# Two small products in separate slots with one PSUM bank each, and the output products spread over six slots

## Chip, cores, metric

One core of a Trainium2 chip. The metric is the device time of one launch in microseconds (us), median of several runs. The experiments ran in several rounds, on more than one chip; each ratio below is to the kernel before in the same rounds.

## The reference, cut

An attention block with 32 inducing points feeds a gated feed-forward layer with a gated residual. `B, N, C = 4, 12416, 128`, `d_ff = 1536`.

```python
h = mab(I, x)                 # 32 summaries of each batch
x = mab(x, h)                 # each token mixes the 32 rows of h
g, val = x @ w_gate, x @ w_val
ffn_out = (gelu(g) * val) @ w_out
out = x + sigmoid(x @ w_res) * ffn_out
```

The kernel never forms the second `x`: it multiplies the attention weights `rt` of each token with matrices that already hold `h @ w_gate`, `h @ w_val`, `h @ w_res` and `h`. What is called a **mix** below is the product of `rt` with the last two: the gate mix gives the argument of the sigmoid, the residual mix gives `x` itself.

## The kernel before

Work goes in groups of 512 tokens. A full group has six **slots**; in each, PE makes two gate halves and two value halves (128 x 512 each), ACT puts a gelu over each gate half, and DVE multiplies 128 x 1024 gelus with the values (`u`). Forty-eight **output products** (128 x 128) then sum `u @ w_out` in one bank, two to seven slots behind the group's start. The last DVE step (`th`) closes the group, POOL adds the residual, and a transfer writes the result.

The eight PSUM banks: three in a ring for gate halves, mixes and small work (`bank_g`), two pairs for values (`bank_v`), one for the output sum (`bank_f`).

```python
p_fin = ctx.enter_context(tc.tile_pool(name="fin", bufs=2))        # th and at
ps_g = ctx.enter_context(tc.tile_pool(name="psg", bufs=3, space=bass.MemoryType.PSUM))
ps_v = ctx.enter_context(tc.tile_pool(name="psv", bufs=2, space=bass.MemoryType.PSUM))
ps_f = ctx.enter_context(tc.tile_pool(name="psf", bufs=1, space=bass.MemoryType.PSUM))
...
def mix(self):
    banks = bank_g(), bank_g()
    n = self.tw
    for k in range(self.nk):
        for r, bank in zip((slice(0, 64), slice(64, 128)), banks):
            pe.matmul(bank[:, k * P:(k + 1) * P],
                      rt_t[self.b, self.k][r, self.j0 + k, :], hra_t[self.b][r, :],
                      start=True, stop=True)
    ...
    act.activation(self.th[:, :n], banks[0][:, :n], AC.Tanh, bias=0.0, scale=0.5)
    ...
    act.activation(self.at[:, :n], banks[1][:, :n], AC.Copy, bias=0.0, scale=1.0)

def end(self):
    ve.scalar_tensor_tensor(self.th[:, :tw], self.th[:, :tw], 1.0,
                            self.ffn.rearrange("p k c -> p (k c)")[:, :tw], AL.add, AL.mult)
    po.tensor_tensor(self.at[:, :tw], self.at[:, :tw], self.th[:, :tw], AL.add)
    ...                                            # sy.dma_start(out..., self.at...)
...
# f: the group's first slot; START, MIDDLE (default), END, LATE order the work behind one slot
at(f + 2, lg.mix, START)
for i, n in enumerate((10, 10, 10, 9, 9)):
    at(f + 3 + i, lambda lg=lg, n=n: lg.mms(n))    # output products
at(f + 7, lg.end, LATE)
```

Beside this runs background work for the next batch: twice per batch a burst of exponentials, after one of which up to 40 accumulation products stand in the slot of the mixes of several groups. The gelus run ahead of the values by some gate halves, their lead; a burst uses it up, and the groups after it make 13 gelus instead of 12 until it has grown again.

The softmax here doesn't subtract the row's maximum and nothing guards it: scores larger than these inputs give would overflow.

## Time and profile before

| | before |
|---|---|
| time, first three runs | 882.23 us (881.86 to 885.05) |
| span of the profiled run | 883.8 us |
| busy: PE, DVE, ACT, POOL | 89%, 90%, 89%, 43% |
| period of a plain group (12 gelus) | 7.85 us, 32 groups |
| period while the gelus' lead grows (13 gelus) | 8.17 us, some 22 groups |
| period with accumulation | 8.66 us |

A period is the time from one start of the last DVE step (L394) to the next, read from the trace; each group has one. The page's slices (40 equal parts of the span, tenths of busy time; PEclk is the clock granted to PE) show where PE ran below full speed:

```profile
PE   5789989999989999899988999999998899999997
...
POOL 2438884112388776111267877311238531111111
PEclk9689989999999999999999999999999899999999
```

The sixth digit of PEclk (110 to 132 us) is an 8, and so is one near 690 us: stretches of half clock. POOL has 8s in slices 4 to 6 (66 to 132 us), while it converts the next batch, and again in slices 12, 13, 23 and 31.

### The profile page before, as it was taken

The page shows a single profiled execution, that of the slowest core. Times are in us where ns is not written, and L with a number is a line of the kernel's source. Part 1 is how long each engine was busy: PE and PEld are TensorE (multiplying, and loading weights), DVE is VectorE, ACT ScalarE, POOL GpSimd, SP SyncE. Part 2 cuts the span into 40 slices and gives each one's busy share as a digit, 9 for nine tenths or more (in the row PEclk, how much of TensorE's full clock was granted, in tenths as well). Part 3 has the DMA queues.
Part 4 walks back from the last instruction along what each step waited for, and adds up shares of the span by engine and source line. Part 5 has one row for each costly group of instructions (what it writes and reads, how often), then busy time and mean ns, then how long its engine had stood idle before and what let it go on. Part 6 is the DMA issues. An engine that isn't in the chain of part 4 may idle for free.

```text
span 883.8 us, 23924 instructions
## 1 busy us (share of the span) xinstructions
PE 787.8 (89%) x9586; PEld 447.7 (51%) x9586; DVE 794.0 (90%) x773; ACT 782.3 (89%) x1462; POOL 380.6 (43%) x376
## 2 busy tenths in 40 slices
PE   5789989999989999899988999999998899999997
PEld 4544445555554445555545544555555454444444
DVE  8679979799799999889888999979979799999998
ACT  5589979799899999889999999989989799999995
POOL 2438884112388776111267877311238531111111
PEclk9689989999999999999999999999999899999999
DMA  8327884001237976100116877200123521101111
GB/s 306 108 76 154 201 191 93 25 26 38 43 78 155 172 196 137 42 26 25 55 38 131 184 182 160 73 36 26 37 43 74 98 62 37 37 26 37 37 37 40
DMA packets 118991, 78.27 MB, mean 89 GB/s; under 512 B 97216, under 2 KB 99936, under 8 KB 118880
## 3 DMA queue, kind: packets, MB, share of 16 engines
q1 hardware_dynamic: 116592, 74.32, 34.4%
q10 hardware_dynamic: 2288, 2.43, 1.0%
q8 instruction: 75, 1.23, 0.6%
q14 instruction: 36, 0.29, 0.1%
HBM read 27.87 MB, written 25.43 MB: 60 GB/s over the span
## 4 chain that ended last, share of the span: by engine, by line
PE 56%; ACT 23%; DVE 13%; issue 4%; DMA 2%; POOL 1%; ACTq 0%; POOLq 0%; SPq 0%; DVEq 0%
PE f L373 25%; PE g L336 22%; ACT ge L342 17%; DVE u L350 10%; ACT th L388 4%; PE v L336 3%; PE g L157 2%; DVE lo L121 2%; ACT at L390 1%; DMA out_dram<-at 1%; DVE hi L119 1%; PE g L175 1%; POOL at L397 1%; PE g L177 1%; ACT L342 0%
## 5 line engine op out<-in xcount | busy, mean ns | idle before, releaser
L350 DVE TENSOR_TENSOR u<-ge,v 128x1024 bf16<-128x1024 f32 x584 | 702.0, 1215 | 71.6 <-PE v L336 33.6
L342 ACT ACTIVATE ge<-g 128x512 f32<-128x512 f32 x1164 | 622.2, 601 | 51.6 <-PE v L336 20.6
L336 PE MATMUL g<-rt,hgv 64*128 64x512 f16 x1152 | 363.1, 386 | 35.9 <-ACT th L388 15.0
L336 PE MATMUL v<-rt,hgv 64*128 64x512 f16 x1152 | 378.6, 389 | 0.4 <-DVE u L350 0.4
L373 PE MATMUL f<-wO,u 128*128 128x128 bf16 x4656 | 350.8, 223 | 1.0 <-DVE th L394 1.0
L373 PEld LDWEIGHTS <-u 128*128 128x128 bf16 x4656 | 267.6, 99 | 165.9 <-issue 164.5
L397 POOL TENSOR_TENSOR at<-at,th 128x512 f32<-128x512 f32 (+1 forms) x100 | 123.7, 1237 | 430.1 <-ACT ge L342 250.1
L336 PEld LDWEIGHTS <-hgv 64*128 64x128 bf16 x2400 | 102.1, 94 | 151.9 <-issue 83.5
L283 POOL TENSOR_TENSOR a<-eb,z 128x1024 f16<-128x1024 f32 (+1 forms) x49 | 90.9, 1862 | 7.3 <-DMA rt<-a 5.5
L384 PE MATMUL g<-hra,rt 64*128 64x128 f16 x768 | 57.6, 218 | 36.1 <-ACT ge L342 31.4
L121 POOL TENSOR_TENSOR lo<-xf,hi 128x1024 f16<-128x1024 f32 x36 | 76.8, 2134 | 0.3
L384 PEld LDWEIGHTS <-rt 64*128 64x128 f16 x768 | 37.3, 94 | 73.9 <-issue 62.7
L394 DVE SCALAR_TENSOR_TENSOR th<-th,f 128x512 f32<-128x512 f32 (+1 forms) x100 | 66.4, 664 | 1.0 <-PE f L373 1.0
L388 ACT ACTIVATE th<-g 128x512 f32<-128x512 f32 (+1 forms) x100 | 58.5, 585 | 5.8 <-PE g L384 5.5
L390 ACT ACTIVATE at<-g 128x512 f32<-128x512 f32 (+1 forms) x100 | 58.1, 581 | 6.1 <-DMA out_dram<-at 5.0
L119 POOL CAST hi<-xf 128x1024 f16<-128x1024 f32 x36 | 37.3, 1037 | 30.3 <-DMA xf<-in_x_dram 26.1
L157 PEld LDWEIGHTS <-xt 128*128 128x128 f16 x768 | 23.3, 98 | 12.1 <-issue 11.7
L137 ACT ACTIVATE xt<-g 128x1024 f16<-128x1024 f16 x12 | 12.3, 1023 | 13.7 <-PE g L136 13.5
L136 PE MATMUL g<-identF,hi 128*128 128x128 f16 x96 | 10.7, 278 | 10.1 <-DVE hi L119 9.9
L261 POOL TENSOR_TENSOR zt<-zt 128x256 f32<-128x256 f32 (+5 forms) x36 | 15.0, 417 | 2.8
L161 ACT ACTIVATE eb<-g 128x512 f32<-128x512 f32 x18 | 9.8, 597 | 5.2 <-PE g L157 5.2
L136 PEld LDWEIGHTS <-hi 128*128 128x128 f16 x96 | 7.9, 125 | 12.4 <-DVE hi L119 12.4
(104 smaller groups left out, 249.0 us busy)
## 6 DMA issues: line engine op xcount, KB each, us to landing
out_dram<-at SPq DMA_DIRECT2D x96, 256.0 KB, 2.1
xf<-in_x_dram SPq DMA_DIRECT2D x42, 512.0 KB, 4.1
ge<-in_x_dram SPq DMA_DIRECT2D x6, 512.0 KB, 6.0
rt<-a SPq DMA_TRANSPOSE x49, 3.1
xt<-hi SPq DMA_TRANSPOSE x36, 3.5
ge<-in_moe_w_gate_dram ACTq DMA_DIRECT2D x1, 512.0 KB, 4.7
ge<-in_moe_w_val_dram ACTq DMA_DIRECT2D x1, 512.0 KB, 5.6
ge<-in_moe_w_out_dram ACTq DMA_DIRECT2D x1, 512.0 KB, 4.3
```

What stands on the lines that cost most here:

```text
L119: e_hi.tensor_copy(hi[:, :w, :], xf[:, :w, :])
L121: e_lo.tensor_tensor(lo[:, :w, :P], xf[:, :w, :], hi[:, :w, :], AL.subtract)
L283: po.tensor_tensor(a2[:, :n], ev[:, o:o + n, :].unsqueeze(2).to_broadcast([P, n, Q, M]), z[:, o:o + n].unsqueeze(2).unsqueeze(3).to_broadc ...
L336: pe.matmul(*t[n], start=True, stop=True)
L342: act.activation(ge_t[i][:, h * TOK:h * TOK + n], gb[:, :n], AC.Gelu, bias=0.0, scale=1.0)
L350: ve.tensor_tensor(u[:, :n], ge_t.pop(i)[:, :n], v_t.pop(i)[:, :n], AL.mult)
L373: pe.matmul(self.ffn[:, k, :], u_t[self.gi, si][:, o:o + P], wO[:, fc, :], start=first, stop=not self.todo, skip_group_check=True)
L384: pe.matmul(bank[:, k * P:(k + 1) * P], rt_t[self.b, self.k][r, self.j0 + k, :], hra_t[self.b][r, :], start=True, stop=True)
L388: act.activation(self.th[:, :n], banks[0][:, :n], AC.Tanh, bias=0.0, scale=0.5)
L390: act.activation(self.at[:, :n], banks[1][:, :n], AC.Copy, bias=0.0, scale=1.0)
L394: ve.scalar_tensor_tensor(self.th[:, :tw], self.th[:, :tw], 1.0, self.ffn.rearrange("p k c -> p (k c)")[:, :tw], AL.add, AL.mult)
L397: po.tensor_tensor(self.at[:, :tw], self.at[:, :tw], self.th[:, :tw], AL.add)
```

## The change

The intent: each mix takes one bank of the ring at a time, so that PE need not wait for two; and the slot of the gate mix, now shorter, takes four of the output products, one slot behind the last output products of the group before. Background work goes ahead of output products.

```diff
-        def mix(self):
-            banks = bank_g(), bank_g()
+        def mix(self, rows):
+            bank = bank_g()
             for k in range(self.nk):
-                for r, bank in zip((slice(0, 64), slice(64, 128)), banks):
-                    pe.matmul(...)
+                pe.matmul(bank[:, k * P:(k + 1) * P], rt_t[self.b, self.k][rows, self.j0 + k, :],
+                          hra_t[self.b][rows, :], start=True, stop=True)
+            return bank[:, :self.tw]
+        def gate(self):       # Tanh of self.mix(slice(0, 64)) into self.th
+        def residual(self):   # Copy of self.mix(slice(64, 128)) into self.at
...
-        at(f + 2, lg.mix, START)
+        at(f + 2, lg.gate, START)
-            for i, n in enumerate((10, 10, 10, 9, 9)):
-                at(f + 3 + i, lambda lg=lg, n=n: lg.mms(n))
+            for i, n in enumerate((4, 9, 9, 7, 9, 10)):
+                at(f + 2 + i, lambda lg=lg, n=n: lg.mms(n), END)
+            at(f + 5, lg.residual, START)
...
-        def bg(g, p, f, where=END):
+        def bg(g, p, f, where=MIDDLE):
```

(Cut: the bodies of `gate` and `residual`, told in the comments; the one-block groups, where the residual goes to `f + 3`; and one `START` of the background work that became the default.)

More of the change, by code (lines that the diff above doesn't have):

```diff
@@ L376, in mms @@
                     del u_t[self.gi, si]
-        def mix(self):
-            banks = bank_g(), bank_g()
-            n = self.tw
+        def mix(self, rows):
+            bank = bank_g()
             for k in range(self.nk):
-                for r, bank in zip((slice(0, 64), slice(64, 128)), banks):
-                    pe.matmul(bank[:, k * P:(k + 1) * P],
-                              rt_t[self.b, self.k][r, self.j0 + k, :], hra_t[self.b][r, :],
-                              start=True, stop=True)
+                pe.matmul(bank[:, k * P:(k + 1) * P], rt_t[self.b, self.k][rows, self.j0 + k, :],
+                          hra_t[self.b][rows, :], start=True, stop=True)
+            return bank[:, :self.tw]
+        def gate(self):
             self.th = p_fin.tile([P, TOK], FP32, name="th", tag="th")
-            act.activation(self.th[:, :n], banks[0][:, :n], AC.Tanh, bias=0.0, scale=0.5)
+            act.activation(self.th[:, :self.tw], self.mix(slice(0, 64)), AC.Tanh,
+                           bias=0.0, scale=0.5)
+        def residual(self):
             self.at = p_fin.tile([P, TOK], FP32, name="at", tag="at")
-            act.activation(self.at[:, :n], banks[1][:, :n], AC.Copy, bias=0.0, scale=1.0)
+            act.activation(self.at[:, :self.tw], self.mix(slice(64, 128)), AC.Copy,
+                           bias=0.0, scale=1.0)
         def end(self):
@@ L515 @@
         f = first[gi]
-        at(f + 2, lg.mix, START)
+        at(f + 2, lg.gate, START)
         if len(groups[gi][4]) == 6:
-            for i, n in enumerate((10, 10, 10, 9, 9)):
-                at(f + 3 + i, lambda lg=lg, n=n: lg.mms(n))
+            for i, n in enumerate((4, 9, 9, 7, 9, 10)):
+                at(f + 2 + i, lambda lg=lg, n=n: lg.mms(n), END)
+            at(f + 5, lg.residual, START)
             at(f + 7, lg.end, LATE)
         else:
-            at(f + 3, lambda lg=lg: lg.mms(len(lg.todo)))
+            at(f + 3, lg.residual, START)
+            at(f + 3, lambda lg=lg: lg.mms(len(lg.todo)), END)
             at(f + 3, lg.end, LATE)
@@ L552, in plan @@
             bg(19, 2, lambda: turn_h(nb))
-            bg(19, 4, lambda: first_layer_t(nb, 0), START)
+            bg(19, 4, lambda: first_layer_t(nb, 0))
             bg(20, 2, lambda: first_layer_t(nb, 1))
```

## The prediction

> **What bounds the kernel now.** I read the page's busy shares first, then the list of waits, then the starts of the last DVE step of each group (L394), one per 512-token group, and last the timeline of single groups.
>
> ```profile
> PE 787.8 (89%) x9586; PEld 447.7 (51%) x9586; DVE 794.0 (90%) x773; ACT 782.3 (89%) x1462; POOL 380.6 (43%) x376
> ```
>
> Three engines at 89 to 90% do not say which is the bound: back-to-back durations overlap. In order of start, ACT steps of 0.6 us follow each other every 0.477 to 0.494 us, and u products of 1.22 us every 1.137 us where nothing is waited for. So a group (12 gelus, two evictions; 6 u, one L394) could take 12 x 0.485 + 2 x 0.485 = 6.8 us on ACT and 6 x 1.137 + 0.597 = 7.42 us on DVE. Between two L394 starts I measure 7.85 us in 32 groups, about 8.17 us in some 22 (there the kernel makes 13 gelus per group to rebuild its lead), 8.66 us in 15 (accumulation beside them), and more around the bursts. Neither engine is at its floor: something with waits paces both.
>
> ```profile
> PE g L384 <- ACT ge L342: 32.6, 98, 0.4
> PE g L336 <- ACT th L388: 15.0, 69, 0.4
> ACT at L390 <- DMA out_dram<-at: 5.0, 4, 1.9
> ```
>
> The list of waits names the suspect: PE waits for ACT at the mixes (L384), once for nearly each of the 100 groups, and then for the gate's eviction (L388). The timeline of a 7.85 us group, PE then ACT then DVE, shows the loop:
>
> ```profile
> 328.54 0.39 PE L336 MATMUL g<-rt,hgv 64*128 64x512 f16 x1
> ...
> 329.08 0.68 PE L373 MATMUL f<-wO,u 128*128 128x128 bf16 x9
> 329.69 0.39 PE L336 MATMUL g<-rt,hgv 64*128 64x512 f16 x1
> ...
> 329.91 0.38 PE L336 MATMUL g<-rt,hgv 64*128 64x512 f16 x1
> ...
> 330.13 0.22 PE L384 MATMUL g<-hra,rt 64*128 64x128 f16 x1
> 330.76 0.38 PE L384 MATMUL g<-hra,rt 64*128 64x128 f16 x7 [0.41 <-ACT ge L342]
> 331.25 0.37 PE L336 MATMUL g<-rt,hgv 64*128 64x512 f16 x1
> ...
> 331.85 0.37 PE L336 MATMUL g<-rt,hgv 64*128 64x512 f16 x1 [0.21 <-ACT th L388]
> ...
> 332.17 0.73 PE L373 MATMUL f<-wO,u 128*128 128x128 bf16 x10
> 332.83 0.39 PE L336 MATMUL g<-rt,hgv 64*128 64x512 f16 x1
> ```
>
> ```profile
> 331.20 0.60 ACT L388 ACTIVATE th<-g 128x512 f32<-128x512 f32 x1
> 331.69 0.59 ACT L390 ACTIVATE at<-g 128x512 f32<-128x512 f32 x1
> ```
>
> ```profile
> 330.41 0.68 DVE L394 SCALAR_TENSOR_TENSOR th<-th,f 128x512 f32<-128x512 f32 x1
> ```
>
> Call slots by place: p0 to p5, p2 the slot of the mixes. Three g banks turn in a ring. At 330.13 the first mix has its bank; the second needs the bank whose gelu ends only at 330.70, so seven products go at 330.76. The next two gate products need the bank of the last gelu (331.19, product at 331.25) and that of th (331.79, product at 331.85). From the p2 start (329.69) to the p4 start (332.83) PE spends 3.14 us; the other four slots run without a wait, 1.202 us with 10 output products and 1.147 with 9: 2 x 1.202 + 2 x 1.147 = 4.70. Sum 7.84, which is the group. PE and ACT in a loop through the banks set the pace, and the two mixes together close that loop.
>
> **What the skill says.** "TensorE: Matmul & The Clock Gate", section "Wait — 56ns, not 53.3ns?": 128 columns warm take 55.6 ns start to start. The trace agrees: a tenth product lengthens a slot by 1.202 - 1.147 = 0.055 us. Same page, "What's actually happening": after about one idle window of 3.4 us the array runs at half rate. Here shorter stretches of waits suffice (next part but one). "PSUM — Partial Sum Buffer", "Terms": two engines may not use a bank in the same partitions at once; so the matmul must wait for the evicting ACT step, as seen. "Perfetto Trace Analysis", "DVE / Act Engine Instruction": the spread of a semaphore comes after the shown end; the trace has 0.06 us (331.79 to 331.85).
>
> **The change, part by part.** The numbers of instructions stay; table loads too (14 in both ACT orders).
>
> *One bank at p2.* The gate mix takes the free bank and goes at once. The residual mix sits in p5, whose third bank is free by then: its gelu began a slot earlier. ACT's second eviction moves out of p2/p3; ACT has slack (6.8 of 7.85).
>
> *Unpaired mixes.* Eight products in two row halves ran beside each other; now 4 and 4. I choose 4 x 0.055 + 0.1 for the changeover = 0.32 us each. The one in p2 lies inside a new wait; the one in p5 is on the path.
>
> *Four output products in p2.* The f bank is single. They must wait for L394 of the group before, which stands on DVE behind the u of p1. That is the new loop. From the p1 start: u starts 0.73 later (328.54 to 329.27), L394 1.137 after that, lasts 0.68, semaphore 0.06; four products and the changeover 4 x 0.055 + 0.115 = 0.335. So p3 starts at 2.94. Then p3 and p4 with 9 products, 1.147 each; p5 with residual and 7: 0.54 + 0.32 + 0.115 + 0.385 = 1.36; p0 with 9: 1.147. Sum 2.94 + 4.80 = 7.74. Without the wait PE would need 1.20 (p1) + 1.20 (p2: 0.54 + 0.32 + 0.335) + 4.80 = 7.20, so some 0.54 us of waiting replaces the old 0.41 + 0.21 and their surroundings. DVE's next u after L394 hides most of it: v of p3 is ready at 2.94 + 0.73 = 3.67, DVE free at 3.60.
>
> So the 7.85 groups gain 0.11. Those with 13 gelus have an unpaired gate product in p1, +0.22: 7.96, for 8.17, gain 0.21. With accumulation (0.7 us, now between gate and outputs, so that it fills the new wait): p2 starts at 1.42, gate ends 2.28, accumulation about 3.1, outputs 3.5, then 4.80: 8.3 for 8.66, gain 0.36.
>
> *The later residual eviction.* at is written three slots (3.6 us) later, so its two buffers have that much longer until the output transfer lands. Today this wait is rare but dear:
>
> ```profile
> 116.96 0.73 PE L373 MATMUL f<-wO,u 128*128 128x128 bf16 x10
> 119.14 0.58 PE L336 MATMUL g<-rt,hgv 64*128 64x512 f16 x1 [1.45 <-ACT at L390]
> ...
> 120.17 1.25 PE L373 MATMUL f<-wO,u 128*128 128x128 bf16 x10
> ```
>
> ACT waited 1.9 us for the transfer, PE 1.45, and then ten products took 1.25 us and not 0.73: the clock had halved, for 6.8 us. That group took 12.20 us, 4.35 over 7.85. Three others sit where the same wait appears, over 7.85 or 8.17 as their neighbours: the one at 685 us loses 4.6, those at 265 and 474 us 0.5 and 1.0. Together 10.4 us. I credit three quarters, 7.8, because th still waits for POOL, whose add of the group two before ended at 115.87, just when th began (115.98); with a faster pace that wait may appear.
>
> Sum: 32 x 0.11 = 3.5; 22 x 0.21 = 4.6; 15 x 0.36 = 5.4; nine groups next to the bursts, at 8.66 to 8.9, 0.25 each = 2.2; stalls 7.8; the six bursts, where the residual no longer holds a bank ahead of the exponentials, 2. Together 25.5, so 882.2 - 25.5 = 857 us.
>
> **Rivals.** *The new wait equals the old.* If u and L394 answer later, or the unpaired mix costs 0.45, the loop is 7.9 and only the stalls and the accumulating groups gain: about 870. For it: the L394 wait lies right behind a full u. Against: each term was read from the trace. *DVE becomes the bound.* If four output products start sooner than I think, the group falls to 7.5, near DVE's 7.42: 96 x 0.3 more, about 838. Against it: 1.137 is seen only between a u and the L394 behind it, so DVE's floor may be higher. *Throttle.* A PE wait of half a microsecond in each group, on top of a burst, could halve the clock more often; seven such times stand in the trace after the start. Each costs 2 to 4 us: up to 866, or with fewer of them 850. *POOL.* In the first eight groups POOL is over 80% busy; the wait on at becomes one on th and saves nothing: +5.
>
> **Range and chances.** The loop's error of 0.1 us times 96 is about 10 us, the stalls' 5: 841 to 872. Faster by 2% means below 864.6: 0.72. Within 2%: 0.26. Slower, only if the throttle spreads: 0.02.
>
> **What would show it.** Right: the mixes no longer wait for ACT's gelu, nor gate products for th; output products wait for the DVE step, some 0.5 us in nearly each plain group; periods 7.74, 7.96 and 8.3; no ACT wait on the output transfer, half clock only after bursts. Wrong: periods of 7.85 with the new wait at 0.6 or more; a wait of the u products on v after p3 or p5; ACT th waiting for POOL; more half-clock stretches.

## The result, and the profile after

The changed kernel takes 855.38 us median (854.61 to 859.1, four runs) against 883.12 (881.86 to 885.05, four runs): ratio 0.9692, interval 0.9658 to 0.9727, faster. A ratio here is the mean time of one kernel's runs over the mean of the other's of the same rounds, so not quite the ratio of the medians quoted. All outputs are right.

In the changed kernel some lines move: the mixes are L381 (L384 before), the gate's ACT step L387 (L388), the residual's L392 (L390), the last DVE step L397 (L394), POOL's add L400 (L397). The busy line and the slices of the page after:

```profile
PE 785.5 (92%) x9586; PEld 471.0 (55%) x9586; DVE 782.7 (92%) x773; ACT 768.2 (90%) x1462; POOL 381.1 (45%) x376
...
PE   5889998999999999899999999999999999999997
...
POOL 2438895112398776111268877311238721111111
PEclk9589999999999999999999999999999999999999
```

The work is the same (the counts agree); the span is shorter, and the two 8s of PEclk inside the main part have gone. The list of waits of the changed kernel (engine and line, what it waited for, us in total, times, longest):

```profile
PE f L373 <- DVE th L397: 36.1, 66, 0.9
...
PE g L336 <- ACT ge L342: 7.8, 10, 1.6
...
ACT th L387 <- POOL at L400: 1.6, 1, 1.6
```

The mixes' wait for ACT (32.6 us before) and the gate halves' wait for the gate's ACT step (15.0) are gone, the latter down to one of 0.8; in their place stands the predicted wait of the output products on the last DVE step, 36.1 us. The wait of the residual's ACT step on the output transfer is gone; one wait on POOL has come.

One plain group in the timeline of PE, then ACT, then DVE (start, us, what):

```profile
324.10 0.39 PE L336 MATMUL g<-rt,hgv 64*128 64x512 f16 x1
...
324.63 0.73 PE L373 MATMUL f<-wO,u 128*128 128x128 bf16 x10
325.30 0.39 PE L336 MATMUL g<-rt,hgv 64*128 64x512 f16 x1
...
325.74 0.38 PE L381 MATMUL g<-hra,rt 64*128 64x128 f16 x4
326.70 0.38 PE L373 MATMUL f<-wO,u 128*128 128x128 bf16 x4 [0.57 <-DVE th L397]
327.01 0.39 PE L336 MATMUL g<-rt,hgv 64*128 64x512 f16 x1
...
329.31 0.39 PE L336 MATMUL g<-rt,hgv 64*128 64x512 f16 x1
...
329.75 0.38 PE L381 MATMUL g<-hra,rt 64*128 64x128 f16 x4
330.07 0.56 PE L373 MATMUL f<-wO,u 128*128 128x128 bf16 x7
330.57 0.39 PE L336 MATMUL g<-rt,hgv 64*128 64x512 f16 x1
```

```profile
326.69 0.60 ACT L387 ACTIVATE th<-g 128x512 f32<-128x512 f32 x1
```

```profile
325.97 0.68 DVE L397 SCALAR_TENSOR_TENSOR th<-th,f 128x512 f32<-128x512 f32 x1
```

The gate mix goes at once (325.74). The four output products stand until the DVE step has ended (325.97 + 0.68 = 326.65) and start at 326.70. From there to the same place in the next group nothing waits for long (the longest, at 330.87, is some 0.08 us).

Where the 30.5 us between the two profiled spans came from, as sums of differences between the periods of the same groups. The timed runs differ by 27.2 us in the mean: the profiled run before took 885.81 us, longer than the four timed ones, at a mean granted clock of 0.969, where the executions in the later rounds show 0.969 to 0.977.

| groups | predicted period | before | after | gain, us | predicted gain |
|---|---|---|---|---|---|
| 32 plain | 7.74 | 7.85 | 7.70 | 3.1 | 3.5 |
| 22 with growing lead | 7.96 | 8.17 | 8.01 | 4.1 | 4.6 |
| 12 with accumulation | 8.3 | 8.66 | 8.40 | 3.1 | 5.4 (for 15) |
| 4 with a transfer stall | | 8.65 to 12.43 | 7.70 to 8.14 | 10.6 | 7.8 |
| 12 around the bursts | | 8.06 to 11.89 | 8.01 to 11.75 | 4.5 | 2 |
| 17 others | | | | 5.1 | 2.2 |

The plain row includes groups 10 and 11, which became 0.22 and 1.03 us longer (the latter, 8.88, by a wait on POOL); the others gain about 0.15 each.

### The profile page after: what moved, and what is told of

Its sections match the earlier page's. It is cut to its first block, busy times and chain, and to the rows that moved or that the text cites.

```text
span 853.3 us, 23930 instructions
## 1 busy us (share of the span) xinstructions
PE 785.5 (92%) x9586; PEld 471.0 (55%) x9586; DVE 782.7 (92%) x773; ACT 768.2 (90%) x1462; POOL 381.1 (45%) x376
## 5 line engine op out<-in xcount | busy, mean ns | idle before, releaser
L350 DVE TENSOR_TENSOR u<-ge,v 128x1024 bf16<-128x1024 f32 x584 | 691.4, 1215 | 55.4 <-ACT ge L342 25.5
L373 PE MATMUL f<-wO,u 128*128 128x128 bf16 x4656 | 360.1, 220 | 36.4 <-DVE th L397 36.1
L336 PE MATMUL v<-rt,hgv 64*128 64x512 f16 x1152 | 367.8, 384 | 0.0
L336 PE MATMUL g<-rt,hgv 64*128 64x512 f16 x1152 | 358.1, 382 | 9.9 <-ACT ge L342 7.8
L400 POOL TENSOR_TENSOR at<-at,th 128x512 f32<-128x512 f32 (+1 forms) x100 | 124.0, 1240 | 397.3 <-DVE th L397 296.2
L336 PEld LDWEIGHTS <-hgv 64*128 64x128 bf16 x2400 | 96.4, 94 | 114.0 <-issue 46.8
L381 PEld LDWEIGHTS <-rt 64*128 64x128 f16 x768 | 56.7, 94 | 48.7 <-issue 13.4
L381 PE MATMUL g<-hra,rt 64*128 64x128 f16 x768 | 73.7, 216 | 0.6
L397 DVE SCALAR_TENSOR_TENSOR th<-th,f 128x512 f32<-128x512 f32 (+1 forms) x100 | 66.5, 665 | 1.0 <-PE f L373 1.0
L387 ACT ACTIVATE th<-g 128x512 f32<-128x512 f32 (+1 forms) x100 | 59.4, 594 | 3.9 <-PE g L381 2.3
L392 ACT ACTIVATE at<-g 128x512 f32<-128x512 f32 (+1 forms) x100 | 59.4, 594 | 3.3 <-PE g L381 3.3
L137 ACT ACTIVATE xt<-g 128x1024 f16<-128x1024 f16 x12 | 12.3, 1025 | 13.5 <-PE g L136 13.5
L161 ACT ACTIVATE ea<-g 128x512 f16<-128x512 f32 x18 | 10.1, 596 | 6.1 <-PE g L157 6.1
```

Source lines behind the costliest of these rows:

```text
L336: pe.matmul(*t[n], start=True, stop=True)
L350: ve.tensor_tensor(u[:, :n], ge_t.pop(i)[:, :n], v_t.pop(i)[:, :n], AL.mult)
L373: pe.matmul(self.ffn[:, k, :], u_t[self.gi, si][:, o:o + P], wO[:, fc, :], start=first, stop=not self.todo, skip_group_check=True)
L381: pe.matmul(bank[:, k * P:(k + 1) * P], rt_t[self.b, self.k][rows, self.j0 + k, :], hra_t[self.b][rows, :], start=True, stop=True)
L387: act.activation(self.th[:, :self.tw], self.mix(slice(0, 64)), AC.Tanh, bias=0.0, scale=0.5)
L392: act.activation(self.at[:, :self.tw], self.mix(slice(64, 128)), AC.Copy, bias=0.0, scale=1.0)
```

## The experiments

Line numbers are those of the kernel that an experiment starts from: mixes L381 and last DVE step L397 where that is the changed kernel, L384 and L394 where it is the kernel before.

**Theory.** The pace before was a loop of PE and ACT through the ring of g banks; the pace after is a loop from p1's value products through `u` and the last DVE step to the four output products in p2 and on to the next p1. A quarter to a third of the gain is a separate matter: the later residual no longer meets an output transfer. **Rivals.** The spreading of output products is what helps; or PE's sum of work sets the pace; or the half clock alone explains the time.

### The split alone

```diff
-            for i, n in enumerate((4, 9, 9, 7, 9, 10)):
-                at(f + 2 + i, lambda lg=lg, n=n: lg.mms(n), END)
+            for i, n in enumerate((10, 10, 10, 9, 9)):
+                at(f + 3 + i, lambda lg=lg, n=n: lg.mms(n))
```

against the changed kernel, with the old order of the background work.

> One part of the change alone: gate mix in p2 and residual mix in p5, one bank each; the output products stay over five slots (10, 10, 10, 9, 9 from p3 on), as before. My theory (the old pace was the loop PE-ACT through the g banks; the new pace is the loop p1 - DVE th - first four output products - p3): without the four products in p2 nothing waits for th before p3's own products, PE needs about 7.1 us, so DVE's floor of 7.42 sets the group: plain groups 7.45 to 7.55, so below the 7.70 of the whole change, and the time about 843 (835 to 850). The wait of the output products on the DVE step stays under 15 us in all. Rival (the spreading over six slots is what brings the gain, the split alone only moves the wait): plain groups 7.8 and more, time 865 to 875.

Measured: 842.58 us (838.49 to 847.09), ratio 0.9554 (0.9507 to 0.9602). Plain groups 7.49, with 13 gelus 7.80, with accumulation 8.28. The list of waits:

```profile
PE g L336 <- ACT ge L342: 18.3, 52, 1.6
...
PE f L373 <- DVE th L397: 0.9, 1, 0.9
```

and DVE in one plain group, here and in the changed kernel (six `u` in a row, their time together):

```profile
317.32 6.98 DVE L350 TENSOR_TENSOR u<-ge,v 128x1024 bf16<-128x1024 f32 x6
324.22 0.68 DVE L397 SCALAR_TENSOR_TENSOR th<-th,f 128x512 f32<-128x512 f32 x1
```

```profile
326.56 7.19 DVE L350 TENSOR_TENSOR u<-ge,v 128x1024 bf16<-128x1024 f32 x6
333.67 0.68 DVE L397 SCALAR_TENSOR_TENSOR th<-th,f 128x512 f32<-128x512 f32 x1
```

DVE is the bound of the first: in the trace it is idle for at most 0.006 us in a plain group (0.11 us in the changed kernel), PE for 0.34 us, waiting for gelus, and the period of 7.49 is near its floor of 7.42. So the split alone does more than the whole change. The four products in p2, with the order of background work that goes with them, give back about 12 us (the ratios differ by 0.0138, of 882 us): they make PE wait for a step that comes behind a full `u`. One group pays for the faster pace: group 11 takes 12.64 us here, behind a wait on POOL (see the last experiment).

### The six slots alone

```diff
-            for i, n in enumerate((10, 10, 10, 9, 9)):
-                at(f + 3 + i, lambda lg=lg, n=n: lg.mms(n))
+            for i, n in enumerate((4, 9, 9, 7, 9, 10)):
+                at(f + 2 + i, lambda lg=lg, n=n: lg.mms(n), END)
```

against the kernel before, whose mixes stay together in p2 (and background work ahead of the output products).

> The other part alone: output products over six slots (4, 9, 9, 7, 9, 10), background work ahead of them; both mixes still together in p2 on two banks. My theory: the bank wait at the mixes stays (some 30 us in all), but it now lies beside the wait for th; p3 begins about 3.1 us after p1, its second gate product waits to 3.36 for the bank of th, then 9, 9, 7, 9 products: plain groups about 7.6 to 7.75. The dear stalls on the output transfer near 115 and 685 us stay, because the residual is still written in p2. Time about 862 (855 to 872). Rival (the split is all that matters): plain groups stay at 7.85, time 875 to 883.

Measured: 863.66 us (861.21 to 865.83), ratio 0.9791 (0.9752 to 0.983). Plain groups 7.62, with accumulation 8.52. PE around the mixes of a plain group, and the waits:

```profile
326.77 0.38 PE L384 MATMUL g<-hra,rt 64*128 64x128 f16 x7 [0.41 <-ACT ge L342]
327.17 0.38 PE L373 MATMUL f<-wO,u 128*128 128x128 bf16 x4
327.49 0.39 PE L336 MATMUL g<-rt,hgv 64*128 64x512 f16 x1
```

```profile
PE g L384 <- ACT ge L342: 32.6, 98, 0.4
...
ACT at L390 <- DMA out_dram<-at: 9.2, 7, 2.1
```

The bank wait is as before, but by its end the DVE step is all but done too, so that the four products have hardly a wait of their own (0.025 us). They fit into time that PE lost anyway: from the seven mixes to the start of p4 PE takes 2.02 us here and 2.07 before, and the slots from p4 to p1 have three products less (0.17 us). In plain groups this part alone is even quicker (7.62) than the whole change (7.70), whose residual mix has come into p5. It loses on the transfer stalls (groups of 10.94 and 9.88 us stay) and on accumulation. So each part alone gains, and the gains do not add. What the new order of background work contributes to this run was not tried apart.

### The kernel before, with a third residual buffer

```diff
-            self.at = p_fin.tile([P, TOK], FP32, name="at", tag="at")
+            self.at = p_fin.tile([P, TOK], FP32, name="at", tag="at", bufs=3)
```

> The kernel before with three buffers for the residual tile in place of two, nothing else. My theory: ACT no longer waits for the output transfer, the stalls of 12.20 and 12.43 us near 115 and 685 us and their stretches of half clock go, plain groups stay at 7.85 and 8.17: time about 873 (870 to 877), that is 8 to 10 us of the 28 gained by the change. Rival (the half clock comes by chance and the transfer wait is no cause): time 880 to 884, and the long groups stay or turn up elsewhere.

Measured: 874.14 us (873.61 to 876.34), ratio 0.9916 (0.9882 to 0.9949). The groups of 12.20 and 12.43 us fall to 7.85 and 8.24, all four stalls together by 9.9 us; plain groups stay at 7.85 and 8.17. The half clock right after those stalls is gone, that after the bursts is not (four stretches of 3.4 us). So the stalls are worth some 7 us by the medians of the same rounds (881.27 before), and the half clock does not explain the rest.

### Products shifted within the loop

```diff
-            for i, n in enumerate((4, 9, 9, 7, 9, 10)):
+            for i, n in enumerate((4, 8, 8, 6, 8, 14)):     # first run
+            for i, n in enumerate((8, 9, 9, 7, 9, 6)):      # second run
```

> The changed kernel with its products shifted towards p1, the slot whose products lie beside the u that th has to wait for anyway: 4, 8, 8, 6, 8, 14 in place of 4, 9, 9, 7, 9, 10. My theory: four products leave the loop (4 x 0.055 = 0.22 us): plain groups 7.48 in place of 7.70, the wait of the output products on th shrinks in share of PE or stays alike, time about 838 to 845. Rival (PE's sum of work sets the group, which is unchanged): 7.70 and 855. Second rival (DVE's floor is higher than 7.42): 7.6 and 848.

> The changed kernel with products moved from p1, outside the loop, into p2, inside it: 8, 9, 9, 7, 9, 6 in place of 4, 9, 9, 7, 9, 10. PE's sum of work is unchanged. My theory (loop p1 - u - DVE th - first products - p3 to p0 - p1): four products more behind th, 4 x 0.055 = 0.22: plain groups 7.92, wait of the output products on th longer than before, time 868 to 874. Rival (PE's total work or DVE alone sets the group): 7.70 and 855.

Measured for 14 in p1: 851.0 us (849.54 to 852.16), ratio 0.9651; plain groups 7.56, so 0.14 less and not 0.22. The time misses what I expected (838 to 845): groups with accumulation rise from 8.40 to 8.51, and group 11 took 11.13 us. PE in a plain group, its wait in p2 and the slot p0:

```profile
320.15 0.38 PE L373 MATMUL f<-wO,u 128*128 128x128 bf16 x4 [0.37 <-DVE th L397]
...
323.87 0.39 PE L336 MATMUL g<-rt,hgv 64*128 64x512 f16 x1
...
324.20 0.37 PE L336 MATMUL g<-rt,hgv 64*128 64x512 f16 x1
```

The two gate halves of p0 start 0.33 us apart, not 0.22 as elsewhere (0.30 in the changed kernel): the residual mix has taken a bank of the ring, so the second half needs the bank of p5's second gelu, which ends at 324.15. The lost 0.08 lies in three places of 0.02 to 0.03 us each, by the starts in the two traces: this wait is longer, p5's mix waits a little for a bank too, and the `u` of p1 starts 0.76 us behind p1 and not 0.73, since DVE still has the `u` before it. DVE is idle for only 0.03 us of the 7.56. The second rival, a higher floor of DVE, would fit this run but not the 7.47 us of the residual mix in p1 (below). In groups with accumulation the four products of p2 follow the accumulation without a wait for the DVE step, so that work moved into p1 is on the path; the 0.11 us more are bank waits in p5, p0 and p1 that shorter slots do not shorten.

Measured for 6 in p1: 873.92 us (872.34 to 875.08), ratio 0.9905 (0.9884 to 0.9926); plain groups 7.93, expected 7.92. The same sum of PE work, 0.23 us more per group than in the changed kernel. PE's sum of work is not the bound; the place of the products is.

### The order of background work

```diff
-                at(f + 2 + i, lambda lg=lg, n=n: lg.mms(n), END)
+                at(f + 2 + i, lambda lg=lg, n=n: lg.mms(n))
-        def bg(g, p, f, where=MIDDLE):
+        def bg(g, p, f, where=END):
```

> The changed kernel with the old order of the background work: in p2 the four output products come ahead of the accumulation, not behind it. My theory: plain groups unchanged at 7.70; in the 15 groups with accumulation the wait for th now stands in front of the 0.7 us of accumulation and not beside it, p3 about 0.4 us later than 8.40: 8.7 to 8.8, time 859 to 863. Rival (the order does not matter): 8.40 and 855.

Measured: 860.8 us (859.74 to 863.4), ratio 0.9761 (0.9739 to 0.9782); groups with accumulation 8.70, plain ones 7.70. As expected: in the changed kernel the accumulation, in front of the output products, fills 0.3 us of the new wait. (Cut from the diff: the same for the one-block groups, and one `START`.)

### The residual mix in p1

```diff
-            at(f + 5, lg.residual, START)
+            at(f + 7, lg.residual, START)
```

> The changed kernel with the residual mix moved from p5, inside the loop, to p1, outside it (beside the u that th waits for). My theory: the 0.32 us of four unpaired products leave the loop, so plain groups fall from 7.70 to DVE's reach, 7.45 to 7.56; groups with accumulation, where PE's sum counts, stay at 8.4 to 8.5; time 845 to 850. Rival (the unpaired mix costs nothing on the path): 7.70 and 855, or more, since the residual tile is later ready for the add.

Measured: 854.53 us (848.26 to 856.12), ratio 0.9672 (0.9632 to 0.9712). Plain groups 7.47, as expected: the residual mix in p5 was in the loop. The total misses (expected 845 to 850): groups with accumulation take 8.61 (expected 8.4 to 8.5), where the mix in p1 waits 0.25 us for a gelu's bank, group 11 takes 12.81 us, and half clock follows three of the bursts (groups of 11.54 to 11.98 us against 10.05). Whether the later residual brings that half clock or chance does, these runs do not settle.

### The split with even slots, and the stall at group 11

```diff
-            for i, n in enumerate((10, 10, 10, 9, 9)):
+            for i, n in enumerate((10, 10, 8, 10, 10)):
```

against the split alone, for the residual mix in p5.

> The split of the mixes alone, with the output products over five slots evened out for the residual mix in p5: 10, 10, 8, 10, 10. The split alone with 10, 10, 10, 9, 9 gave plain groups of 7.49 and 842.6 us, with DVE's u products 1.131 us apart but 1.214 behind p5. My theory (DVE bound, its floor 7.42): 7.43 to 7.50, at most 5 us less: 837 to 844. Rival (PE's work still bounds it): no change in plain groups.

Measured: 841.41 us (839.8 to 847.43), ratio 0.9549. Plain groups 7.50, not lower than the 7.49 of the split alone: no gain is shown. That is what the rival forecast, but its reason, PE's work, does not hold: DVE is never idle in these groups, while PE is for 0.34 us. Its PE timeline shows what the faster pace brought, at group 11, just ahead of a burst:

```profile
136.66 0.73 PE L373 MATMUL f<-wO,u 128*128 128x128 bf16 x10
140.61 0.46 PE L336 MATMUL g<-rt,hgv 64*128 64x512 f16 x1 [3.21 <-ACT th L387]
...
141.63 1.25 PE L373 MATMUL f<-wO,u 128*128 128x128 bf16 x10
```

ACT stood 3.67 us until POOL had made an add that was queued behind conversions for the next batch; PE stood, and its clock halved (ten products in 1.25 us, not 0.73). A third buffer for the gate tile, then for both:

```diff
-            self.th = p_fin.tile([P, TOK], FP32, name="th", tag="th")
+            self.th = p_fin.tile([P, TOK], FP32, name="th", tag="th", bufs=3)
-            self.at = p_fin.tile([P, TOK], FP32, name="at", tag="at")
+            self.at = p_fin.tile([P, TOK], FP32, name="at", tag="at", bufs=3)   # second run only
```

> The split with 10, 10, 8, 10, 10 (841.4 us) and a third buffer for the gate tile. In that kernel's trace the gate's ACT step waits 3.67 us for POOL's add of the group two before, once, near 136 us; PE then stands still for 3.21 us, its clock halves, and the group takes 12.38 us against 7.5. My theory (the wait on POOL that I named as a rival has appeared at the faster pace): with three buffers the wait goes and the group falls to about 7.8, time 4 to 5 us less: 836 to 838, ratio to the kernel before about 0.949. Rival (POOL itself is late and the wait moves to the residual tile or to another group): 840 to 842, the long group stays or turns up at the next groups.

Measured: 841.37 us (836.51 to 844.2), ratio 0.9536 (0.9505 to 0.9566). The rival was right: the wait moved. ACT now waited for output transfers in the residual's step (4.9 us in three waits), and groups 9 to 12 took 8.60, 8.18, 10.41 and 10.44 us.

> The run before it, with a third buffer for the residual tile as well. With three gate buffers alone the wait moved to the residual tile: ACT waited 1.24, 0.79 and 2.83 us for output transfers in groups 9 to 11 (periods 8.60, 8.18, 10.41 against 7.50), and the time stayed at 841.4. My theory (POOL catches up within a few groups, so that three buffers of both are enough): groups 9 to 11 fall to 7.5 to 8, about 4 us less: 835 to 838.5. Rival (POOL's backlog before the burst is longer than any buffer and comes out as a wait for its converted tiles or at the burst): 840 to 842.

Measured: 835.43 us (834.46 to 836.13), ratio 0.9457 (0.9432 to 0.9481). Groups 9 to 11 take 7.50 us each, and the profiled run has no half clock between 52 us and its last 3 us. This is the best version: the split, no output products in p2, three buffers for both tiles.

## Why the prediction was right

**The old loop** was read rightly. With the two banks taken apart, the waits of 32.6 and 15.0 us vanished; with the mixes left together they stayed at 32.6, and output products put into them shortened the group to 7.62.

**The new loop** closed as told: 7.70, 8.01 and 8.40 measured for 7.74, 7.96 and 8.3 (with accumulation p2 starts 1.53 behind p1 and not 1.42, since the 13th gate product waits for a bank). Term by term in the plain group shown: p1 start to `u` 0.73 (same), the DVE step 1.138 behind it, 0.05 to the products, then p3 after 0.31 (told 0.335). Two sizes were off and cancelled by luck. p5 took 330.57 - 329.31 = 1.26, not 1.36: the unpaired mix cost 0.22 on the path, not 0.32. p0 took 1.24, not 1.147: its second gate half waits some 0.08 for the bank of p5's second gelu (done at 330.82, start at 330.87), because the residual mix has taken one turn of the ring; I had found no bank wait there. The doses in p1 and p2 confirm the loop: four products into it cost 0.23, four out of it gave 0.14.

**The stalls** on the transfer went, and more fully than credited: the four groups gain 10.6 us, some 0.6 of it by the faster pace, where I had taken 7.8 of 10.4. (The 10.4 is a slip: the group at 685 us has neighbours of 8.17 and so loses 4.3, not 4.6.) The third buffer shows their worth by itself, 9.9 us in its trace and about 7 us of medians.

**The sum** came near partly by luck. The paces gave 11.6 us for the 13.5 told (3.1, 4.1 and 4.4), and other terms made up for it. The accumulation was counted for 15 groups; 12 have it, and three more have the step that closes the summaries and appear among the others with 1.3 us. Around the bursts 4.5 us came where I told 2, but not for the reason told. One stretch of half clock (3.4 us) follows a burst in the profiled run, where five did before; that is worth some 5 us, an estimate from groups in the same place where none fell (8.06 for 9.57 us, and 10.26 for 11.31 with the third residual buffer). Without it the bursts gained nothing: the groups of the first bursts took 10.17 us for 9.54, three times, those of the second 11.75 for 11.89. How much of the half clock the change took away is not settled.

**The rivals.** "DVE becomes the bound" did not happen in the changed kernel but does in the split alone: 7.49. (Its sum was wrong: 96 x 0.3 us below 857 is 828, not 838.) "POOL" came as one wait of 1.6 us at group 11, which made that group 8.88 us; it grows to 3.67 us at the faster pace. "The new wait equals the old" was wrong by 0.15 us a group.

**What I did not see:** that the four products in p2 were the dear part. My own numbers had it: PE needed 7.20 without the wait and 7.74 with it.

## What to carry to other kernels

When three engines are each 90% busy, look at the spacing of back-to-back instructions rather than their durations, and add up one period start to start: the bound may be a loop of waits through a ring of banks. Work placed behind a wait on a late step makes a new loop; ask of each piece moved whether it lands inside or beside the loop, and try the part of a change that removes a wait without the part that adds one. When the pace rises, a tile's two buffers that were enough may not be: single stops of PE of 1.45 and 3.21 us made their groups 4.35 and 4.9 us longer here, and half clock came with both.

## What the Trainium skill lacked or had wrong

- "TensorE: Matmul & The Clock Gate", "What's actually happening": it ties the fall to half rate to an idle window of about 3.4 us. Here PE stood 1.45 us in one piece (before, from 117.7 us), and half rate began within it, at 118.6 us, for 6.8 us; ten products took 1.25 us in place of 0.73. No section says how short a stop can do it.
- "Perfetto Trace Analysis", "DVE / Act Engine Instruction": it tells which part of an instruction the window covers. Beyond a general overhead for each memory, the skill has no overlap for a DVE product like this one, which reads PSUM and SBUF and writes bf16 to SBUF. Here `u` products of 1.21 to 1.22 us repeat every 1.131 us, so 0.08 to 0.09 us of each is hidden; a sum of durations would put DVE nearer to its limit than it is.
